# A six-layer cross network: the first group's row chunks loaded in halves, and its tails turned together on column tiles

## The chip, the cores and the metric

The kernel runs on 1 core of one Trainium2 chip. The metric is device time of one execution, in microseconds (us); less is better. A profiled execution also has a span, from its first to its last instruction, which is about 1.8 us shorter than the time.

## The reference

```python
B, F, D, L = 16384, 26, 16, 6;  Din = 416          # bf16
def reference(x0, ws, bs):
    x = x0
    for l in range(L):
        proj = jnp.einsum('bd,de->be', x, ws[l]) + bs[l]
        x = x0 * proj + x
    return x
```

## The kernel before

The kernel keeps features on the partitions, so x0 is transposed. The batch is cut into 8 groups of 2048 rows, a group into 4 chunks of 512. The 416 features are three tiles of 128 and a tail of 32; the tails of the four chunks stand under each other in one tile of 128 partitions. Groups 1 to 6 are transposed by transposing DMAs. In the kernel before, group 1's are issued from 6.44 us and its tail rows have landed at 22.53; group 0 is loaded as plain rows (issued from 0.73 us, all landed at 10.41) and turned by the tensor engine (a matmul with an identity), into PSUM, from where ScalarE and VectorE copy it to SBUF. A small scheduler derives every semaphore wait from what each instruction reads and writes; for PSUM it knows only whole banks. A write to one half of a bank waits for a read of the other half.

The parts that matter, before the change:

```python
    load_nat(0, 0, 2)                  # chunk 0 in halves, first queue ("sp")
    load_nat(0, 2, KK)
    load_wm(0, "sp")                   # weight block 0, 3 x 128 rows
    for j in range(1, NJ):
        load_nat(j, 0, KK)             # chunks 1 to 3, whole
    load_w3(0, "sp")                   # 4 copies of the last 32 weight rows, 26 KB each
    load_group(1, lambda: load_wm(1, "sp"))   # group 1: transposing DMAs
    ...
    def transposed_chunk(j):
        ba, bb = ((0, 1), (3, 0), (1, 3), (0, 1))[j]       # two PSUM banks
        first = (0, P, 2 * P, D - P)                       # three tiles and the tail
        seq = [(t, k) for t in range(NT) for k in range(KK)]        # chunk 0: by halves
        for n, (t, k) in enumerate(seq + [(NT, k) for k in range(KK)]):
            ...                                            # 16 transposes of 128 x 128
        # ScalarE copies tiles 0 and 1 (bank ba); VectorE tile 2 and the tail (bank bb)

    def first_job():
        transposed_chunk(0)
        ...                            # bias turned and copied
        keep_busy(8, 3)                # filler matmuls
        full(g, l, 0, ba, ..., chunks=[0]);  full(g, l, 1, bb, ..., chunks=[0])
        transposed_chunk(1)
        transposed_chunk(2)
        full(g, l, 0, ba, ..., chunks=[1])
        transposed_chunk(3)
        load_w3(1, "act")
        full(g, l, 1, bb, ..., chunks=[1])                 # the dense stretch starts here
        full(g, l, 0, ba, ..., chunks=[2, 3])
        rows32(g, l, 0, ba, False)                         # first use of the tails
        ...
```

## Time and profile before

| | value | view |
|---|---|---|
| time | 477.25 us, median of 3 (476.77 to 478.11) | runs |
| tensor engine busy | 462.2 us, 97% | page |
| weight block 0 landed | 5.46 us | semaphores in the trace |
| chunks 1, 2, 3 landed | 7.88, 9.42, 10.41 us | semaphores in the trace |
| first use of the tails (L477) | 14.03 us | timeline |

Two lines of the page of the kernel before: the busy times of the engines with their instruction counts, and the shares of the chain of work that ended last:

```profile
PE 462.2 (97%) x3325; PEld 195.7 (41%) x3379; DVE 404.0 (85%) x696; ACT 342.4 (72%) x372; POOL 6.8 (1%) x15
...
PE 95%; issue 1%; DMA 1%; ACT 1%; DVE 1%; SPq 0%
```

The tensor engine (PE) bounds the kernel, so what counts is when its unbroken work starts. The tensor engine's timeline of the kernel before; the columns are start, us from first start to last end, engine, line, operation, output and inputs, shape, count, and in brackets the idle time before it and who ended it:

```profile
5.81 1.24 PE L456 MATMUL ps<-x,wm 128*128 128x512 bf16 x5 [0.25 <-ACT x L565]
7.92 1.07 PE L561 MATMUL ps<-ident,x 128*128 128x128 bf16 x16 [0.87 <-DMA x<-in_x_dram]
9.56 1.05 PE L561 MATMUL ps<-ident,x 128*128 128x128 bf16 x16 [0.57 <-DVE x L568]
10.45 0.81 PE L456 MATMUL ps<-x,wm 128*128 128x512 bf16 x3
11.10 1.06 PE L561 MATMUL ps<-ident,x 128*128 128x128 bf16 x16
12.21 1.89 PE L456 MATMUL ps<-x,wm 128*128 128x512 bf16 x8
14.03 0.40 PE L477 MATMUL ps<-x,w 32*128 32x512 bf16 x4
```

L561 are the transposes of chunks 1, 2 and 3, L456 the dense matmuls (one of the six and one of the nine have no record). Two idles stand out, 0.87 and 0.57 us, both before transposes. The second is put down to a VectorE copy. The instruction waits for two things, the landing of chunk 2 and an older VectorE copy that ended at 5.66 us; chunk 2 landed at 9.42, so the load was the releaser. The chain of waits of the kernel before says the same of the first: from 2.13 to 7.88 us it is one load.

```profile
2.13 5.75 DMA x<-in_x_dram
```

### The profile page before, as it was taken

Reading aid. Unit: us, or ns where it says so; the run is one execution under the profiler, and the core shown is the slowest. Engines: PE = TensorE matmul, PEld = TensorE weight load, DVE = VectorE, ACT = ScalarE, POOL = GpSimd, SP = SyncE. Lnnn points to the kernel's source line nnn. Section 1 sums busy time; section 2 is a strip of 40 time slices with the busy share of each in tenths; the row PEclk is TensorE's granted clock in tenths of the full one; section 3 lists DMA queues with packets and bytes.
Section 4 is the critical chain, followed back from the end, with each engine's and each line's share of the span. In section 5 each row is a group of like instructions: output and inputs, shape, how many; then the busy total and the mean of one; then the engine's idle time right before and its main releaser. Section 6 shows DMA issues by size and latency. Waiting matters only on the chain.

```text
span 475.7 us, 8355 instructions
## 1 busy us (share of the span) xinstructions
PE 462.2 (97%) x3325; PEld 195.7 (41%) x3379; DVE 404.0 (85%) x696; ACT 342.4 (72%) x372; POOL 6.8 (1%) x15
## 2 busy tenths in 40 slices
PE   7999999999999999999999999999999999999995
PEld 6344444444444444444444444434444444444442
DVE  2888888888888888898889869988888888888896
ACT  4677777777777777777777777777777777777785
POOL 1000000000000000000000000000000000000000
PEclk9999999999999999999999999999999999999999
DMA  8866950640002397369308940990000039025899
GB/s 223 181 150 137 190 113 1 142 81 1 28 7 44 63 228 158 76 139 244 84 21 195 208 108 9 178 279 2 1 10 25 4 64 242 15 45 117 227 155 288
DMA packets 138363, 53.31 MB, mean 112 GB/s; under 512 B 112330, under 2 KB 137428, under 8 KB 138324
## 3 DMA queue, kind: packets, MB, share of 16 engines
q1 hardware_dynamic: 137848, 52.46, 49.2%
q8 instruction: 26, 0.43, 0.4%
q10 hardware_dynamic: 476, 0.32, 0.2%
q14 instruction: 13, 0.11, 0.1%
HBM read 5.97 MB, written 13.63 MB: 41 GB/s over the span
## 4 chain that ended last, share of the span: by engine, by line
PE 95%; issue 1%; DMA 1%; ACT 1%; DVE 1%; SPq 0%
PE ps L456 77%; PE ps L477 7%; PE ps L497 6%; PE ps L798 2%; DMA x<-in_x_dram 1%; PE ps L471 1%; ACT tw L394 1%; PE ps L561 1%; PE ps L488 1%; DVE x L864 0%; PE ps L809 0%; ACT x L852 0%; DVE x L858 0%; PE ps L841 0%; SPq L521 0%
## 5 line engine op out<-in xcount | busy, mean ns | idle before, releaser
L394 ACT ACTIVATE tw<-ps,bias 128x1024 bf16<-128x1024 f32 (+1 forms) x295 | 299.8, 1071 | 119.8 <-PE ps L477 80.7
L456 PE MATMUL ps<-x,wm 128*128 128x512 bf16 x1638 | 371.7, 379 | 5.8 <-issue 3.7
L456 PEld LDWEIGHTS ps<-x,wm 128*128 128x128 bf16 x1692 | 158.9, 98 | 213.5 <-issue 27.9
L403 DVE TENSOR_TENSOR tw<-tw,x 128x1024 bf16<-128x1024 bf16 (+1 forms) x285 | 192.3, 682 | 52.8 <-ACT tw L394 52.4
L408 DVE TENSOR_TENSOR x<-tw,x 128x1024 bf16<-128x1024 bf16 (+1 forms) x285 | 183.0, 682 | 0.0
L477 PE MATMUL ps<-x,w 32*128 32x512 bf16 x512 | 39.2, 379 | 0.0
L497 PE MATMUL ps<-x,wm 128*32 128x512 bf16 x564 | 33.0, 380 | 0.0
L434 ACT ACTIVATE ts<-ps,bias 128x512 bf16<-128x512 f32 x47 | 28.8, 701 | 0.0
L438 DVE TENSOR_TENSOR x<-ts,x 128x512 bf16<-128x512 bf16 x47 | 18.6, 417 | 3.7 <-DMA x<-x 3.6
L497 PEld LDWEIGHTS ps<-x,wm 128*32 128x32 bf16 x564 | 13.8, 96 | 17.6 <-issue 5.3
L477 PEld LDWEIGHTS ps<-x,w 32*128 32x128 bf16 x512 | 7.8, 92 | 27.6 <-issue 27.1
L436 DVE TENSOR_TENSOR ts<-ts,x 128x512 bf16<-128x512 bf16 x47 | 18.5, 417 | 0.0
L666 POOL COPY ost<-ot 128x512 bf16<-128x512 bf16 x6 | 5.4, 898 | 423.7 <-DMA ot<-x 423.7
L798 PE MATMUL ps<-wm,x 128*128 128x416 bf16 x48 | 9.5, 340 | 0.0
L852 ACT ACTIVATE x<-ps 128x416 bf16<-128x416 f32 x16 | 7.7, 533 | 2.0 <-PE ps L798 1.9
L568 DVE COPY x<-ps 128x512 bf16<-128x512 bf16 x4 | 1.7, 424 | 8.7 <-PE ps L561 8.7
L565 ACT ACTIVATE x<-ps 128x512 bf16<-128x512 bf16 x8 | 4.3, 594 | 5.6 <-PE ps L561 5.6
L798 PEld LDWEIGHTS ps<-wm,x 128*128 128x128 bf16 x48 | 4.3, 98 | 4.2 <-issue 1.0
L561 PE MATMUL ps<-ident,x 128*128 128x128 bf16 x64 | 4.6, 226 | 1.4 <-DMA x<-in_x_dram 0.9
L858 DVE TENSOR_TENSOR x<-x,x 128x832 bf16<-128x832 bf16 (+1 forms) x10 | 5.0, 504 | 1.1 <-ACT x L852 1.1
L488 PE MATMUL ps<-x,w 32*32 32x512 bf16 x188 | 5.9, 374 | 0.0
L471 PE MATMUL ps<-x,w 32*32 32x512 bf16 x208 | 5.6, 385 | 0.0
(38 smaller groups left out, 35.7 us busy)
## 6 DMA issues: line engine op xcount, KB each, us to landing
out_dram<-ost SPq DMA_DIRECT2D x6, 1664.0 KB, 7.1
x<-in_x_dram SPq DMA_DIRECT2D x7, 416.0 KB, 8.0
x<-x SPq DMA_DIRECT2D x24, 96.0 KB, 2.2
wm<-in_ws_dram SPq DMA_DIRECT2D x6, 312.0 KB, 3.7
out_dram<-ost SPq DMA_DIRECT2D x2, 832.0 KB, 6.7
x<-x SPq DMA_DIRECT2D x22, 64.0 KB, 2.0
out_dram<-x SPq DMA_DIRECT2D x3, 416.0 KB, 3.6
x<-ost SPq DMA_DIRECT2D x28, 32.0 KB, 2.2
```

The lines of the kernel that those rows point to most:

```text
L394: add("act", lambda h, a=a, w=w, b0=b0: h.activation(tw[r][:, a * CH:(a + w) * CH], psum[:, b0 * CH:(b0 + w) * CH], ACT_F.Identity, bias=b ...
L403: add("dve", lambda h, a=a, e=e: h.tensor_tensor(tw[r][:, a * CH:e * CH], tw[r][:, a * CH:e * CH], x0s[s0][:, i * GC + a * CH:i * GC + e * ...
L408: add("dve", lambda h, a=a, e=e: h.tensor_tensor(xs[so][:, i * GC + a * CH:i * GC + e * CH], tw[r][:, a * CH:e * CH], src(i, a, e), ALU.ad ...
L434: add("act", lambda h: h.activation(ts[r][:, :], bank(b), ACT_F.Identity, bias=bias[:, 3, l:l + 1], scale=1.0), reads=[("ps", b), "bias"], ...
L436: add("dve", lambda h: h.tensor_tensor(ts[r][:, :], ts[r][:, :], x03, ALU.mult), reads=[("ts", r)] + tok0, writes=[("ts", r)], release=True)
L438: add("dve", lambda h: h.tensor_tensor(x3s[so][:, :], ts[r][:, :], res, ALU.add), reads=[("ts", r)] + rtok, writes=[("x3", so), ("x3", so, ...
L456: add("pe", lambda h, t=t, j=j: h.matmul(bank(banks[j]), wm[l][:, t, ecols], src(t, j, j + 1), start=(first and t == 0), stop=(not first a ...
L471: add("pe", lambda h, q=q, j=j, r=r, c=c, o=o: h.matmul(psum[o, banks[j] * CH:(banks[j] + 1) * CH], w3[l][q, i * P + c * T32:i * P + (c + ...
L477: add("pe", lambda h, q=q, j=j, r=r: h.matmul(bank(banks[j]), w3[l][q, ecols], src[q, :], start=first, stop=not first, tile_position=(r * ...
L488: add("pe", lambda h, l=l, b=b, s3=s3, ri=ri, qi=qi, ro=ro, qo=qo: h.matmul(psum[qo, b * CH:(b + 1) * CH], w3[l][qi, NT * P:D], s3[qi, :], ...
L497: add("pe", lambda h, t=t, j=j, src=src, l=l, b=b, ro=ro, qo=qo: h.matmul(psum[qo, b * CH:(b + 1) * CH], wm[l][:, t, NT * P:D], src(t, j, ...
L798: add("pe", lambda h, t=t: h.matmul(bank(b, n=D), xcol(t, j, kk), wm[l][:, t, :], start=(first and t == 0), stop=(not first and t == NT - 1)),
```

## The change

Its intent: let the tensor engine start on half a chunk; drop the fourth round of 128-wide transposes in each chunk, and turn all tails at the end with 32-wide ones, four side by side; save three VectorE copies; let ScalarE and VectorE copy chunk 0 at once; and take load issues off the first queue. The diff, cut:

```diff
     for j in range(1, NJ):
-        load_nat(j, 0, KK)
-    load_w3(0, "sp")
+        load_nat(j, 0, 2)
+        load_nat(j, 2, KK)
+    load_w3(0, "act", range(3))
+    load_w3(0, "sp", range(3, NJ))
 ...
     def transposed_chunk(j):
         ba, bb = ((0, 1), (3, 0), (1, 3), (0, 1))[j]
-        seq = [...]                        # tile by tile, the tail last
+        place = ((ba, 0), (bb, 0), (ba, CH)) if j == 0 else ((ba, 0), (ba, CH), (bb, 0))
+        for k2 in (0, 2):                  # by halves in every chunk
+            for t in range(NT):
+                for k in (k2, k2 + 1):
+                    transpose tile t, block k into place[t]
 ...
+    def transposed_tails(b):
+        for k in range(KK):
+            for j in range(NJ):            # column tile j: partitions 32j to 32j+31
+                add("pe", ... psum_t(b)[o, CH + k * P:CH + (k + 1) * P], x0n[:, j, k, NT * P:D],
+                    is_transpose=True, tile_position=(0, j * T32))
+        add("dve", one copy of 128 x 512)
 ...
-        keep_busy(8, 3)
+        keep_busy(5, 3)
 ...
         transposed_chunk(3)
+        transposed_tails(1)
```

More of the change, by code (lines that the diff above doesn't have):

```diff
@@ L281, in load_wm, with load_w3 @@
             writes=[("wm", l)], lane=f"wm{l}", batch=0)
-    def load_w3(l, eng):
-        for j in range(NJ):
+    def load_w3(l, eng, js=range(NJ)):
+        for j in js:
             add(eng, lambda h, j=j: h.dma_start(w3[l][j * T32:(j + 1) * T32, :], ws[l, NT * P:D, :]),
@@ L551, in transposed_chunk @@
         s = slot(0)
-        first = (0, P, 2 * P, D - P)
-        seq = [(t, k) for t in range(NT) for k in range(KK)]
-        if j == 0:
-            seq = [(t, k) for k2 in (0, 2) for t in range(NT) for k in (k2, k2 + 1)]
-        for n, (t, k) in enumerate(seq + [(NT, k) for k in range(KK)]):
-            if j == 0 and n == NT * 2:
-                keep_busy(2, 3)
-            b, o = (ba, t * CH) if t < 2 else (bb, (t - 2) * CH)
-            c = slice(o + k * P, o + (k + 1) * P)
-            add("pe", lambda h, t=t, k=k, b=b, c=c: h.transpose(
-                psum_t(b)[:, c], x0n[:, j, k, first[t]:first[t] + P], ident[:, :]),
-                reads=[("nat", j, k), x0_tok(nat, 0, 0), "ident"], writes=[("ps", b)])
@@ L564, in transposed_chunk @@
-        for t in range(2):
-            add("act", lambda h, t=t: h.activation(
-                x0s[s][:, cols(t, j)], psum_t(ba)[:, t * CH:(t + 1) * CH], ACT_F.Copy),
-                reads=[("ps", ba)], writes=[x0_tok(s, t, j)])
-        add("dve", lambda h: h.tensor_copy(x0s[s][:, cols(2, j)], psum_t(bb)[:, 0:CH]),
-            reads=[("ps", bb)], writes=[x0_tok(s, 2, j)])
-        q = slice(j * T32, (j + 1) * T32)
-        add("dve", lambda h: h.tensor_copy(x0s[s][q, XW:XW + CH], psum_t(bb)[P - T32:P, CH:2 * CH]),
-            reads=[("ps", bb)], writes=[("x03q", s, j)])
+        place = ((ba, 0), (bb, 0), (ba, CH)) if j == 0 else ((ba, 0), (ba, CH), (bb, 0))
@@ new lines, in transposed_chunk @@
+        for k2 in (0, 2):
+            for t in range(NT):
+                b, o = place[t]
+                for k in (k2, k2 + 1):
+                    c = slice(o + k * P, o + (k + 1) * P)
+                    add("pe", lambda h, t=t, k=k, b=b, c=c: h.transpose(
+                        psum_t(b)[:, c], x0n[:, j, k, t * P:(t + 1) * P], ident[:, :]),
+                        reads=[("nat", j, k), x0_tok(nat, 0, 0), "ident"], writes=[("ps", b)])
+            if j == 0 and k2 == 0:
+                keep_busy(2, 3)
@@ new lines, in transposed_chunk @@
+        for t in range(NT):
+            b, o = place[t]
+            dst, sp_ = x0s[s][:, cols(t, j)], psum_t(b)[:, o:o + CH]
+            kw = dict(reads=[("ps", b)], writes=[x0_tok(s, t, j)])
+            if b == bb:
+                add("dve", lambda h, dst=dst, sp_=sp_: h.tensor_copy(dst, sp_), **kw)
+            else:
+                add("act", lambda h, dst=dst, sp_=sp_: h.activation(dst, sp_, ACT_F.Copy), **kw)
+    def transposed_tails(b):
+        s = slot(0)
+        for k in range(KK):
+            for j in range(NJ):
+                o = slice(j * T32, (j + 1) * T32)
+                add("pe", lambda h, j=j, k=k, o=o: h.matmul(
+                    psum_t(b)[o, CH + k * P:CH + (k + 1) * P], x0n[:, j, k, NT * P:D], ident[:, :],
+                    is_transpose=True, tile_position=(0, j * T32)),
+                    reads=[("nat", j, k), x0_tok(nat, 0, 0), "ident"], writes=[("ps", b)])
+        add("dve", lambda h: h.tensor_copy(x0s[s][:, XW:XW + CH], psum_t(b)[:, CH:2 * CH]),
+            reads=[("ps", b)], writes=x03_toks(s))
```

## The prediction

> **What bounds the kernel.** The tensor engine. The page gives it 462.2 us busy of a 475.7 us span (97%), the chain that ended last is 95% tensor engine, and the list of waits shows few tensor waits after 14 us, none over 0.4 us. The change touches only the first 14 us, so it is worth what it does to the moment at which the dense matmuls start (12.0 us, in the timeline of the tensor engine), and that shift should pass nearly whole to the end.
>
> **That start-up, before.** The first matmul waits for weight block 0, which lands at 5.46 us. Six matmuls then end near 6.9. Chunk 1 lands at 7.88 (wait 0.87 us), chunk 2 at 9.42 (0.57), chunk 3 at 10.41. Of the sixteen shares of chunk 1 fifteen land by 6.51, one at 7.88. Transposes issue every 0.056 us, 16 in 0.9 us; two ScalarE copies take 1.09 us, a VectorE copy 0.42.
>
> **What the change does.**
> 1. Chunk 0 on two engines: worth nothing, because the first matmul still waits for the weights at 5.46, and the next wait is for chunk 1.
> 2. Halves: transposes can begin about half a chunk (8 packets of 131 ns, so about 0.5 us) sooner. The same bytes move; the last half lands no earlier, perhaps 0.2 us later, as three small weight loads (six 39 ns packets per DMA engine) now come ahead. [...]
> 3. The half order brings tile 2 of chunks 2 and 3 to position 5 of 12. It writes the bank that ScalarE is still copying from the chunk before; the tensor engine now waits for that copy. I reckon about 0.3 to 0.8 us of wait before chunk 2's and chunk 3's tile 2. Before, eight transposes ran ahead of that wait and it cost nothing.
> 4. Tails: 16 transposes (0.9 us of tensor time, 0.45 of it in chunks 2 and 3, where it counts) become 16 column-tiled ones. [...]with 4 at once I estimate 0.22 us. VectorE saves three copies of 0.43 us, off the critical path. But the tails go to the other half of the bank that holds chunk 3's tile 2, right after its last transpose: the tensor engine must wait for pipeline end (0.2) plus VectorE copy (0.42), about 0.65 us idle.
>
> Walking the dependencies with these durations: chunk 2's transposes end near 10.1 (before 10.45), chunk 3's near 11.85, tails begin near 12.5, and the dense matmuls start near 12.8 instead of 12.0: 0.8 us later. If the late sixteenth share vanishes, both kernels start sooner, the new one still later.
>
> **Time.** 477.25 plus 0.8 is 478.05; I allow for errors of my walk and for hidden slack and say 477.8 us, range 476.4 to 479.0. Chance of faster by over 2%: 0.01; within 2%: 0.98; slower: 0.01.
>
> **What shows each step.** Timeline of the tensor engine: first L456 matmul still at 5.5 to 5.8; chunk 1's transposes begin sooner (7.3 or earlier); gaps released by ScalarE copies in chunks 2 and 3; a gap near 0.65 us released by VectorE before the column-tiled transposes, which take 0.2 to 0.4 us; the first L456 after them near 12.8. Group 1's tail rows (landed 22.53, used 22.78) not later than now.
>
> **What would make it wrong.** Halves landing over 1 us sooner; weight loads stalling ScalarE's queue past 4.5 us, delaying its first copy (slower); group 1's transposing loads coming earlier or later; run-to-run spread (476.77 to 478.11) larger than the effect.

The 0.22 us of item 4 is an estimate, the 0.9 us of item 4 with four transposes at once; in the trace of the kernel before, the four column-tiled transposes of the bias (L586) start 3 to 4 ns apart, from 4.822 to 4.832 us.

## The result, and the profile after

The changed kernel takes 478.34 us, median of 6 (478.02 to 478.84); the kernel before, 477.5, median of 6 (476.64 to 478.11). The ratio is 1.002, with a 95% interval of 1.0007 to 1.0034. Ratios and intervals differ by up to 0.0003 (in e2_t2last) from those of the plain means of the runs, which the text gives in us. In means the change costs 0.96 us: within 2%, but clear of noise.

The page of the changed kernel, busy times and chain, as above:

```profile
PE 462.3 (97%) x3322; PEld 195.4 (41%) x3376; DVE 402.9 (85%) x693; ACT 342.4 (72%) x372; POOL 6.5 (1%) x15
...
PE 95%; ACT 2%; issue 1%; DMA 1%; DVE 1%; SPq 0%
```

VectorE has three copies less (693 instructions, 402.9 us), the tensor engine is as busy as before, and ScalarE has gone from 1% to 2% of the chain. The tensor engine's timeline of the changed kernel, same columns (again one matmul of the six and one of the nine have no record, so the dense stretch starts at 12.98, one matmul of 0.216 us before 13.20):

```profile
6.62 1.46 PE L456 MATMUL ps<-x,wm 128*128 128x512 bf16 x5 [0.87 <-DMA wm<-in_ws_dram]
7.91 1.06 PE L560 MATMUL ps<-ident,x 128*128 128x128 bf16 x16
9.80 0.62 PE L560 MATMUL ps<-ident,x 128*128 128x128 bf16 x8 [0.84 <-ACT x L572]
10.26 0.81 PE L456 MATMUL ps<-x,wm 128*128 128x512 bf16 x3
10.91 0.39 PE L560 MATMUL ps<-ident,x 128*128 128x128 bf16 x4
11.49 0.62 PE L560 MATMUL ps<-ident,x 128*128 128x128 bf16 x8 [0.20 <-ACT x L572]
12.63 0.41 PE L580 MATMUL ps<-ident,x 128*32 128x128 bf16 x16 [0.52 <-DVE x L570]
13.20 1.89 PE L456 MATMUL ps<-x,wm 128*128 128x512 bf16 x8 [0.16 <-issue]
15.02 0.40 PE L477 MATMUL ps<-x,w 32*128 32x512 bf16 x4
```

The waits for chunk loads are gone: chunk 1's halves landed at 7.02 and 7.52 us and its transposes (L560) follow the matmuls without a gap. In their place stand 0.84 and 0.20 us for ScalarE copies and 0.52 us for a VectorE copy. The chain of waits of the changed kernel shows where the path runs now:

```profile
1.66 4.82 DMA wm<-in_ws_dram
...
8.66 1.09 ACT x L572 x2
9.76 0.05 issue
9.80 0.52 PE ps L560 x6
10.33 0.02 issue
10.35 1.09 ACT x L572 x2
11.45 0.04 issue
11.49 0.64 PE ps L560 x8
12.13 0.02 issue
12.15 0.44 DVE x L570
12.59 0.04 issue
12.63 0.41 PE ps L580 x16
```

It starts at weight block 0, which landed at 6.48 us (before: 5.46), then alternates between transposes and ScalarE copies, and passes through VectorE before the tails. L477 starts at 15.02 instead of 14.03 us, 0.99 later; the span is 476.7 instead of 475.7 us. The shift is handed through to the end.

### The profile page after: what moved, and what is told of

Its sections match the earlier page's. It is cut to its first block, busy times and chain, and to the rows that moved or that the text cites. A ratio compares the mean times of both kernels' runs of the same rounds, so it can differ in the third digit from the quotient of the medians.

```text
span 476.7 us, 8347 instructions
## 1 busy us (share of the span) xinstructions
PE 462.3 (97%) x3322; PEld 195.4 (41%) x3376; DVE 402.9 (85%) x693; ACT 342.4 (72%) x372; POOL 6.5 (1%) x15
## 3 DMA queue, kind: packets, MB, share of 16 engines
HBM read 5.97 MB, written 13.63 MB: 41 GB/s over the span
## 4 chain that ended last, share of the span: by engine, by line
PE 95%; ACT 2%; issue 1%; DMA 1%; DVE 1%; SPq 0%
PE ps L456 77%; PE ps L477 7%; PE ps L497 6%; PE ps L812 2%; DMA wm<-in_ws_dram 1%; PE ps L471 1%; ACT tw L394 1%; PE ps L488 1%; ACT x L572 0%; PE ps L560 0%; DVE x L878 0%; PE ps L823 0%; ACT x L866 0%; DVE x L872 0%; PE ps L855 0%
## 5 line engine op out<-in xcount | busy, mean ns | idle before, releaser
L456 PE MATMUL ps<-x,wm 128*128 128x512 bf16 x1638 | 371.9, 379 | 6.6 <-issue 3.8
L456 PEld LDWEIGHTS ps<-x,wm 128*128 128x128 bf16 x1692 | 158.9, 98 | 214.3 <-issue 27.9
L477 PE MATMUL ps<-x,w 32*128 32x512 bf16 x512 | 39.2, 379 | 0.0
L477 PEld LDWEIGHTS ps<-x,w 32*128 32x128 bf16 x512 | 7.8, 92 | 27.6 <-issue 27.5
L560 PE MATMUL ps<-ident,x 128*128 128x128 bf16 x48 | 4.4, 243 | 1.0 <-ACT x L572 1.0
```

What stands on the lines that cost most here:

```text
L456: add("pe", lambda h, t=t, j=j: h.matmul(bank(banks[j]), wm[l][:, t, ecols], src(t, j, j + 1), start=(first and t == 0), stop=(not first a ...
L477: add("pe", lambda h, q=q, j=j, r=r: h.matmul(bank(banks[j]), w3[l][q, ecols], src[q, :], start=first, stop=not first, tile_position=(r * ...
```

## The experiments

One number turned out to be enough to read each trace by: the start of the first L477. In eight of the fourteen traces the span is 461.65 to 461.73 us longer than that start, in two 461.8; the other four (e5, e9, e10, e12) have a later wait, told below. The table has, for each profiled run, the landing of weight block 0, the first L477, the span, and the mean time against the kernel before of the same rounds.

| run | block 0 landed | first L477 | span | mean time less before's | 95% interval of the ratio |
|---|---|---|---|---|---|
| before, first trace | 5.46 | 14.03 | 475.7 | | |
| changed kernel | 6.48 | 15.02 | 476.7 | +0.96 | 1.0007 to 1.0034 |
| e1_tails7 | 5.90 | 14.08 | 475.7 | +1.01 | 1.0008 to 1.0034 |
| e2_t2last | 6.61 | 15.70 | 477.5 | +1.44 | 1.0009 to 1.0044 |
| e3_w3late | 5.80 | 14.34 | 476.0 | +0.71 | 1.0003 to 1.0027 |
| e4_all3 | 5.41 | 13.52 | 475.2 | +0.08 | 0.999 to 1.0014 |
| e5_best | 5.78 | 13.78 | 476.6 | +1.41 | 1.0018 to 1.0043 |
| e6_t2w3late | 5.80 | 13.63 | 475.4 | +0.21 | 0.9992 to 1.0019 |
| e7_before, second trace | 5.94 | 13.40 | 475.1 | (one look) | |
| e8_before_w3 | 5.72 | 12.97 | 474.6 | (one look) | |
| e9_w3timed | 5.95 | 13.74 | 475.8 | 0.00 | 0.9986 to 1.001 |
| e10_new | 6.57 | 14.99 | 477.0 | -0.23 | 0.9979 to 1.0008 |
| e11_whole | 6.22 | 14.50 | 476.2 | +0.62 | 0.9998 to 1.0027 |
| e12_fill | 6.70 | 13.55 | 475.8 | -0.09 | 0.9983 to 1.0014 |

My theory was the prediction's: the order by halves and the tails' bank make the tensor engine wait for copies. Rivals: the landing of the loads decides; or the switch to column tiles costs it. The first three runs undo one cause each, the fourth all three together.

### The tails in a bank of their own

```diff
-        transposed_tails(1)
+        transposed_tails(7)
```

> One part altered: the column-tiled tails are written to bank 7 (free since the bias copy) instead of the other half of bank 1. Theory A (bank conflict): the 0.52 us idle before the column-tiled transposes, released by the VectorE copy, goes away; dense matmuls (first of the nine after the tails) start near 12.3 us instead of 12.98, span 0.6 to 0.7 us shorter than the changed kernel. Rival B[...]: the idle before the tails stays at 0.3 us or more.

The end of its start-up in the tensor engine's timeline:

```profile
11.14 0.62 PE L560 MATMUL ps<-ident,x 128*128 128x128 bf16 x8 [0.19 <-ACT x L572]
11.69 0.41 PE L580 MATMUL ps<-ident,x 128*32 128x128 bf16 x16
12.03 2.12 PE L456 MATMUL ps<-x,wm 128*128 128x512 bf16 x9
```

The 0.52 us are gone. The wait was the shared bank, not the switch to column tiles: theory A. But the switch is not free. By the starts of the single instructions, the first column tile comes 0.149 us after the transpose before it, and the first matmul 0.152 us after the last tile, where transposes of one shape follow each other every 0.056; so each switch costs about 0.1 us, which the timeline doesn't list as idle because the instruction before is still shown as running. The sixteen tiles themselves start within 0.19 us. The dense stretch starts at 12.03 (expected 12.3), 0.95 us before the changed kernel's; 0.36 of that was there at chunk 1's transposes already (7.55 against 7.91), as block 0 landed sooner, and 0.59 is the tails'. The timed gain is not seen: the mean is +1.01 us, or +0.73 without one run of 479.42. With intervals of about 0.6 us either way, the timed runs cannot confirm 0.7 us for this part alone.

### Tile 2 last

```diff
-        for k2 in (0, 2): for t in range(NT): for k in (k2, k2 + 1): ...
+        if j > 0:
+            seq = [(t, k) for k2 in (0, 2) for t in range(2) for k in (k2, k2 + 1)] + [(2, k) for k in range(KK)]
```

> One part altered: in chunks 1 to 3 the order is tiles 0 and 1 by halves, then tile 2 with all four, so that eight transposes stand ahead of the bank that ScalarE still copies from. Theory A: the waits of 0.84 and 0.20 us for ScalarE before tile 2 shrink to at most 0.7 in sum; ScalarE's copy of chunk 2 starts when its copy of chunk 1 ends (near 9.6 instead of 10.35), chunk 3's transposes end near 11.3 instead of 11.95; dense start near 12.3, span about 0.6 us shorter than the changed kernel. Rival B (landing of the halves decides, not the bank): transposes still end near 11.9 and the span does not move.

The timeline lists no wait for ScalarE any more (0.11 us of idle are left before chunk 2's tile 2, less than it lists), but the span is 0.8 us longer than the changed kernel's. The tensor engine's timeline of this run:

```profile
6.75 2.31 PE L456 MATMUL ps<-x,wm 128*128 128x512 bf16 x6 [1.60 <-DMA wm<-in_ws_dram]
8.84 2.64 PE L563 MATMUL ps<-ident,x 128*128 128x128 bf16 x24
```

Six matmuls take 2.31 us instead of 1.46, and 24 transposes 2.64 us: until 10.6 us one every 0.107 us, twice the 0.056 of the other traces. Three windows of the same run; the columns are busy times of the engines, then the granted tensor clock, DMA share and GB/s:

```profile
3.80:7.20 3.40, 1.80 (x27) 1.28 (x25) 0.42 (x1) 1.17 (x3) 0.44 (x1) 1.00 1.01 326
7.20:10.60 3.40, 3.40 (x22) 2.30 (x21) 0.23 (x1) 0.66 (x2) 0.00 (x0) 0.50 1.19 252
10.60:14.00 3.40, 2.77 (x43) 1.83 (x41) 1.27 (x4) 2.58 (x5) 0.00 (x0) 1.00 1.11 208
```

After a stretch in which the engine idled 1.60 us waiting for block 0 (busy 1.80 of 3.40), the clock was 0.50 from 7.20 to 10.62 us by the clock records. So the run neither confirms nor refutes the theory. Its six times fall in two heaps, 477.35 to 477.62 and 479.29 to 479.76; two of the upper three have a mean clock of 0.994, the third 1.0.

The moment of the full clock differs from run to run: it is first recorded at 3.84 us in the kernel before, 5.09 in the changed one and 3.79 to 10.03 in the others, and the one half-clock stretch between two full ones lasted 3.41 us. What decides the moment was not shown.

### The small weight loads later

```diff
-    load_w3(0, "act", range(3))
     load_w3(0, "sp", range(3, NJ))
 ...                                   # in first_job, after the bias copy
+        load_w3(0, "act", range(3))
```

> One part altered: the three small weight loads on ScalarE's queue are issued after the bias copy instead of at 1.4 us. Theory A (they come ahead of weight block 0 and delay it): block 0 lands by 5.6 us instead of 6.48 and the first dense matmul starts by 5.7 instead of 6.4; but the start of the dense stretch moves by less than 0.3 us, because ScalarE's copies of chunk 1 and the bank waits stand between, so the span is within 0.3 us of the changed kernel. Rival B (one lagging DMA engine by chance): block 0 lands late in some runs whatever the order.

From its timeline of the tensor engine:

```profile
5.94 1.46 PE L456 MATMUL ps<-x,wm 128*128 128x512 bf16 x6 [0.19 <-DMA wm<-in_ws_dram]
...
12.29 2.12 PE L456 MATMUL ps<-x,wm 128*128 128x512 bf16 x9
```

Block 0 landed at 5.80 and the first matmul started at 5.94 (expected: by 5.6 and 5.7); the bank idles are as before (0.84, 0.20 and 0.52 us). Theory A failed at the dense stretch: it was to move by less than 0.3 us and moved by 0.69 (12.29 against 12.98), the whole of the 0.68 by which the first matmul came sooner. The waits for copies don't soak up a late block 0, because the copies come later with it. So of the 0.99 us between the first traces of the two kernels 0.68 hang on when block 0 landed in that one trace of the changed kernel. The mean time is 0.25 us nearer to the kernel before's than the changed kernel's was, well inside the intervals. Whether the early loads delay block 0 is taken up below with more traces.

### All three

The edits of the three runs above, together.

> The three alterations together. By the same walk of dependencies the dense stretch starts near 10.9 to 11.5 us (kernel before: 11.99, changed kernel: 12.98). If nothing else binds, the span is 0.5 to 1.1 us shorter than the kernel before. But group 1's tail rows land at 22.4 to 22.5 us and are wanted at 22.78 in the kernel before, so I expect a new wait there and a gain over the kernel before of only 0.3 to 0.5 us.

Its timeline of the tensor engine, from the second wait on:

```profile
9.13 0.40 PE L562 MATMUL ps<-ident,x 128*128 128x128 bf16 x4 [0.51 <-ACT x L572]
...
10.78 0.41 PE L580 MATMUL ps<-ident,x 128*32 128x128 bf16 x16
11.12 2.12 PE L456 MATMUL ps<-x,wm 128*128 128x512 bf16 x9
13.52 0.40 PE L477 MATMUL ps<-x,w 32*128 32x512 bf16 x4 [0.28 <-DMA w<-in_ws_dram]
```

The dense stretch starts at 11.12, about 0.9 us before that of the kernel before's first trace (11.99, if the one matmul without a record ran just ahead of the eight recorded). Of this 0.28 us is given back at once: the small loads, now issued after the bias copy, landed only at 13.47. I had expected the new wait at group 1's tail rows; they landed at 22.01 and were used at 22.27, so that wait did not come. Timed, the loss is gone (mean +0.08 us, interval 0.999 to 1.0014), but there is no gain either, where 0.3 to 0.5 us had been expected.

One comparison isolates the two bank waits in timed runs. This kernel differs from e3_w3late in nothing but the two bank edits (tile 2 last, tails in bank 7), and both ran in the same rounds on the same chip: 476.70 to 477.60 us against 477.61 to 477.95, five runs each without overlap, 0.63 us apart in the mean. Together the two waits do cost time, though each edit alone could not show it.

### Tile 2 last with the small loads later

The edits of e2_t2last and e3_w3late; the tails stay in bank 1.

> Changed kernel with tile 2 last and the small weight loads late, tails still in bank 1. The run with tile 2 last alone lost the tensor clock for one window (7.20 to 10.62 us at half) after an idle of 1.6 us before weight block 0. Theory A: with block 0 early there is no such idle, the clock stays granted, the ScalarE waits before tile 2 stay at or under 0.5 us in sum, only the 0.52 us wait for the VectorE copy before the tails remains; dense start near 11.6, span about 1.2 us shorter than the changed kernel. Rival B: tile 2 last itself costs as much as it saves; dense start stays at 12.3 or later.

Two lines of its list of waits, tensor engine, first 30 us; the columns are who waited for what, us in total, times, longest (left out: the wait of the first fillers for their input):

```profile
PE ps L580 <- DVE x L570: 0.5, 1, 0.5
PE ps L562 <- ACT x L572: 0.3, 1, 0.3
```

The clock was kept (1.00 from 7.20 to 10.60 us, six matmuls in 1.46 us), the ScalarE wait is 0.33 us, the dense stretch starts at 11.59 and the span is 1.2 us shorter than the changed kernel's, as theory A expected. Timed, the mean is +0.21 us against the changed kernel's +0.96, so about three quarters of the loss went with these two edits, as far as intervals of 0.6 us let one say.

### A second trace of the kernel before

No edit.

> The kernel before, unchanged, for a second trace of it. If the late sixteenth share of chunk 1 (7.88 us against 6.51 for the fifteenth) belongs to the kernel, it is there again, over 1 us late; if it was chance, the shares lie within 0.8 us of each other, chunk 1 is landed by 7.0 and the dense stretch starts near 11. [...]

Its timeline of the tensor engine:

```profile
7.58 1.50 PE L561 MATMUL ps<-ident,x 128*128 128x128 bf16 x24
9.36 0.62 PE L561 MATMUL ps<-ident,x 128*128 128x128 bf16 x8 [0.28 <-ACT x L565]
```

The late share did not come again: chunk 1 landed at 7.02, its fifteenth share at 6.79 (first trace: 7.88 and 6.51). The sixteen lie 1.06 us apart, not within 0.8, and the dense stretch starts at 11.36, not near 11. Neither 0.87 nor 0.57 us of waiting for loads is there. So the two idles that the halves were to remove belonged in large part to one execution; a wait for chunk 1 can come without a late share, though: e9_w3timed below, with whole chunks, has one of 0.37 us. L477 starts at 13.40, 0.63 us sooner than in the first trace, and the changed kernel's loss looks larger against it; e4_all3's dense stretch at 11.12 is ahead of this one by only 0.24 us.

### The small weight loads on the second queue, alone

```diff
-    load_w3(0, "sp")
+    load_w3(0, "act", range(3))
+    load_w3(0, "sp", range(3, NJ))
```

This is the kernel before with that part of the change alone. First:

> One part of the change alone on the kernel before: three of the small weight loads on ScalarE's queue from 1.4 us. Theory A: weight block 0 lands at 5.9 us or later (5.9 to 6.6 in the three traces with these loads early; 5.4 to 5.8 in the three without) and the first dense matmul starts at 6.0 or later. Rival B (chance): block 0 lands by 5.6.

Block 0 landed at 5.72, between the two expectations. Its span was the shortest of all traces, so it was timed:

> The same kernel as the one look with the small weight loads alone (three of them on ScalarE's queue, everything else as before), now timed. Its first trace was the shortest yet (span 474.6, dense start 10.93). Theory A (this part alone is a gain, as it takes three issues off the first queue and three loads from behind chunk 3): 0.4 to 0.8 us faster than the kernel before in the mean. Rival B (its one look was a lucky one): within 0.3 us.

Rival B: the ratio is 0.9998 (0.9986 to 1.001). The early loads cost the kernel before nothing that the interval shows (about 0.6 us either way), and gain it nothing. (In its trace group 1's tail rows made the engine wait 0.30 us.) Over all traces block 0 landed at 6.28 us in the mean of the seven with early loads (5.72 to 6.70) and at 5.77 in the mean of the seven without (5.41 to 6.22). The ranges overlap, so a delay of about 0.5 us is likely but a single trace cannot show it. The three loads are six packets of 39 ns on each DMA engine, 0.23 us; that is an estimate from the packets, and would explain half.

### Halves undone

In e6_t2w3late, whole chunks are loaded again:

```diff
-        load_nat(j, 0, 2)
-        load_nat(j, 2, KK)
+        load_nat(j, 0, KK)
```

> The run with tile 2 last and late small loads, with whole chunk loads in place of halves. Theory A (halves are worth nothing, as chunk 1's first half lands before the tensor engine is free for it): dense start within 0.3 us of that run's 11.6, time within 0.3 us of it. Rival B (halves bring 0.5 us, as I predicted for the start of the transposes): dense start at 12.0 or later and 0.4 us or more slower.

The dense stretch started at 12.09, 0.50 us later, and the mean is 0.41 us higher: by their numbers, rival B. But its cause is not shown to be the halves: the first matmul came 0.42 us later (6.35 against 5.93), because block 0 landed at 6.22; only 0.20 us is a wait for chunk 2. A further 0.29 us went at L477 on the last of the small weights, which landed at 14.36 (in e6_t2w3late at 11.32). The times, +0.62 and +0.21, come from two chips and their intervals overlap. What halves are worth stays open; a few tenths in favour of them is possible.

### Trying to beat both

First with the small loads on the first queue between chunks 1 and 2, and group 1's big weight load moved to ScalarE's queue:

```diff
+        if j == 1:
+            load_w3(0, "sp")
-    load_group(1, lambda: load_wm(1, "sp"))
+    load_group(1)
 ...  # with tails in bank 7, tile 2 last, keep_busy(8, 3)
+        load_wm(1, "act")
```

> Tails in bank 7, tile 2 last, the four small weight loads on the first queue between chunks 1 and 2 (so behind weight block 0, ahead of the transposing loads), eight filler matmuls again instead of five, and group 1's big weight load moved to ScalarE's queue so that its tail rows are issued 0.6 us sooner. Theory: weight block 0 lands by 5.6, dense start 10.7 to 11.2 us, no wait for the small weights (0.28 us in the run with the three alterations), group 1's tail rows land by 21.9; span 474.6 to 475.2, 0.5 to 1.1 us shorter than the kernel before. If group 1's chain binds instead, its tail rows are landed less than 0.3 us before the matmul that uses them and the gain stays under 0.5.

Its timeline near group 1:

```profile
22.21 1.04 PE L456 MATMUL ps<-x,wm 128*128 128x512 bf16 x4 [0.47 <-DMA x<-in_x_dram]
23.69 0.61 PE L477 MATMUL ps<-x,w 32*128 32x512 bf16 x8 [0.45 <-DMA x<-ost]
```

It was the slowest version but one. The dense stretch started at 11.74, after 0.71 us of waiting for a half of chunk 2, and then group 1 bound: the first queue began its transposing loads at 6.89 us (changed kernel: 5.82), its tail rows landed at 23.64 (22.36), and the tensor engine waited 0.47 and 0.45 us. The small loads ahead of them on the first queue are the likely cause, but group 1's big weight load moved to the other queue in the same run, so their part is not shown.

Then with whole chunks, tile by tile, and with tile 2 of chunks 2 and 3 in banks 7 and 6, so that no transpose shares a bank with a running copy:

```diff
-        ba, bb = ((0, 1), (3, 0), (1, 3), (0, 1))[j]
+        ba, bb = ((0, 1), (3, 0), (1, 7), (0, 6))[j]
-        transposed_tails(1)
+        transposed_tails(7)
 ...  # early small loads as in the change, load_wm(1, "act"), keep_busy(8, 3)
```

> Small weight loads on ScalarE's queue, whole chunk loads, transposes tile by tile, tile 2 of chunks 2 and 3 in banks 7 and 6 (which nothing else uses then), column-tiled tails in the free half of bank 7, eight fillers, group 1's big weight load on ScalarE's queue. Theory: no wait for ScalarE or VectorE between chunk 1 and the dense stretch, dense start 10.2 to 10.6 us (set by the landing of chunk 3), group 1's tail rows landed by 21.0; span 474.0 to 474.5, about 1 us shorter than the kernel before in the mean. If group 1's transposing loads bind instead, the gain stops at 0.5 us and a wait shows before group 1's first tiles near 19 to 22 us.

Its profiled run has its first record of the full clock at 10.03 us and was the slowest of its six:

```profile
6.70 2.72 PE L456 MATMUL ps<-x,wm 128*128 128x512 bf16 x6 [0.44 <-DMA wm<-in_ws_dram]
```

The six matmuls took 2.72 us instead of 1.46, and the dense stretch began at 12.94, not 10.2 to 10.6. Between chunk 1 and it there is indeed no wait over 0.15 us, for loads or for copies. After L477 its activations came late: ScalarE issued loads until 16.07 us and began its next activation at 16.11, and the tensor engine waited 0.16 us for it before 17.28. The other five spans are 474.9 to 475.6. The mean is -0.23 us with an interval of 0.9979 to 1.0008: not a proven gain. Last, the same with more fillers before the first matmul:

```diff
-        keep_busy(8, 3)
+        keep_busy(12, 3)
```

> The last version with twelve fillers in place of eight before the first dense matmul. In its profiled run the full tensor clock came only at 10.03 us, after an idle of 0.44 us before weight block 0, and that run was the slowest of six (span 477.0; the five others 474.9 to 475.6). Theory[...]: no run of this one is over 476.2 in span, the mean is 0.4 to 0.8 us below the kernel before of the same rounds, and where the clock is full early the dense stretch starts at 10.3 to 11.0 us. Rival (chance decides, or the fillers only delay the first matmul): a run over 476.5 shows again, or the mean is within 0.3 us of the kernel before.

No run was over 475.8 in span, but the mean is within 0.1 us of the kernel before, which is the rival's case. Block 0 landed at 6.70, so that even twelve fillers left 0.73 us idle. The full clock was there from 5.12 us all the same, so a single idle of that length did not take it here. The dense stretch started at 11.51, and group 1's tail rows then made the engine wait 0.23 us:

```profile
22.85 0.61 PE L477 MATMUL ps<-x,w 32*128 32x512 bf16 x8 [0.23 <-DMA x<-ost]
```

No version beat the kernel before clear of noise.

## Why the prediction was right, and where its steps were off

The prediction said 477.8 us and 476.4 to 479.0; the median is 478.34. Its walk of the dependencies said 0.8 us later at the dense stretch, the traces show 0.99 us at L477, the timed means 0.96.

That the walk's 12.8 lies so near the measured 12.98 is in part luck. It let the first matmul start at 5.5 to 5.8 and kept the late share of chunk 1; in the changed kernel's trace the first matmul came at 6.62 and no share of chunk 1 was late, two errors that pull opposite ways. In e3_w3late, with the first matmul at 5.94, nearly as foretold, the dense stretch started at 12.29, half a microsecond before the walk's, and only 0.3 after that of the kernel before's first trace. The loss in the timed means does not rest on that luck: e3_w3late's is +0.71, of which the two bank edits remove 0.63. Step by step:

1. *Chunk 0 on two engines, worth nothing.* Held in the changed kernel's trace: ScalarE's copies ended at 6.20 us and block 0 landed at 6.48. But block 0 was to land at 5.5, and there it would have been a tie: in the kernel before, ScalarE's copies ended at 5.53 and block 0 landed at 5.46, so the first matmul waited last for ScalarE, not for the weights, by 0.07 us. The part was never run alone.
2. *Halves start the transposes about 0.5 us sooner.* The halves did come (7.02 and 7.52), but chunk 1's transposes began at 7.91, as before, since the matmuls ahead of them waited for block 0 until 6.62. "First L456 matmul still at 5.5 to 5.8" was wrong. I had reckoned the small loads' delay for the chunks and left it out for block 0.
3. *0.3 to 0.8 us of wait before tile 2.* Measured 0.84 and 0.20 us; they fell to 0.33 and none when tile 2 went last with the clock kept (e6_t2w3late), and to 0.51 and none in e4_all3. Shown in the traces.
4. *Tails: 0.22 us of work and 0.65 us of idle.* The idle is 0.52 us by the timeline, which counts from the end of the last transpose; the foretold 0.65 includes that end and compares with 0.68 (0.74 from start to start, less the usual 0.056). It vanished with another bank (e1_tails7). Shown. The work was taken too small, because the two switches between full-width work and column tiles were left out: in e1_tails7 0.49 us pass from the last transpose's start to the first matmul's, so on the path the column tiles save next to nothing of the 0.45 us that they replace. In the trace the four tiles of a round start 3 to 4 ns apart, and each switch adds about 0.1 us (0.149 and 0.152 us instead of 0.056).
5. *The shift passes whole to the end.* Shown by the constant 461.65 us after L477 in both traces. Group 1's tail rows landed at 22.36 us (before: 22.53), not later, as foretold.

One premise was weaker than I wrote. The waits for chunks 1 and 2 in the kernel before were read from one execution with a late DMA share. In its second trace they are absent (and in e9_w3timed one of 0.37 us is there), so the change had less to win than its own profile suggested. No gain from taking issues off the first queue is shown either: in e9_w3timed, with three of the small loads issued from ScalarE's queue, the first queue began group 1's loads at 4.20 us instead of 6.44, and the time changed by 0.00 us.

What stays open: how the 0.63 us that the two bank edits save together are split between tile order and tails, and what the rest of the 0.96 us is, since the intervals are as wide as the parts; the worth of halves; whether the early small loads really delay block 0; and the part of the five fillers in place of eight, which no run undid alone (in the kernel before's second trace the eight ran until the first matmul at 6.28, 0.34 us after block 0 had landed).

## What to carry to other kernels

Before reordering transposes to meet a load sooner, list which PSUM bank each one writes and who is still copying from that bank: an order that follows the data can run into a copy that the old order had hidden behind eight other transposes (0.84 and 0.20 us of waiting here). Give a short extra result a bank that nobody is reading, not the spare half of one that was just filled, where the dependencies are kept by whole banks as here (0.52 us of waiting in bank 1, none in bank 7). And look at two traces before you set out to remove a start-up wait: a late DMA share of one execution (1.37 us after the fifteenth in the first trace, 0.23 in the second) looks just like a property of the kernel.

## What else the traces show

- In the kernel before, transposes of 128 x 128 ran one every 0.107 us, 314 ns long, until the first record of the full clock at 3.84 us, and one every 0.056 us, 219 ns long, after it.
- In e2_t2last the half clock came after 3.40 us with 1.80 us busy and one idle of 1.60 us; in the changed kernel a single idle of 0.87 us was not followed by it. How much idle time it takes is not shown.
- A tile of 32 rows (L477) starts 0.312 us after a matmul of 512 columns in the dense stretch, where the next full matmul starts after 0.216 (medians of 65 and 1556 cases, the same in the kernel before and the changed one): about 0.1 us more.
- In the changed kernel the three load issues on ScalarE's queue went out from 1.40 to 2.66 us, during the table load of 1.28 us (from 1.33) and all begun before the small activation at 2.63 us; both stand ahead of them in the program.
